# The last sections of a fused Fourier-mixing and attention kernel: output-projection chains issued two at a time on half the partitions each

## The chip, the cores and the metric

The kernel runs on one core of one Trainium2 chip. The metric is the device time of one launch in microseconds (us): the median of three runs is 1662.59, and they lie between 1661.75 and 1662.68. The core has five engines with an instruction queue each: TensorE (PE, matmuls, with weight loads shown apart as PEld), VectorE (DVE), ScalarE (ACT), GpSimd (POOL) and SyncE (SP, which here only issues transfers). Each queue runs in order.

## The reference

Two mixers work on the same 2048 x 512 input and are blended row by row with a gate.

```python
def _A_ref(x, dft_seq_re, dft_seq_im, dft_hid_re, dft_hid_im):
    a = jnp.einsum("bsd,ed->bse", x, dft_hid_re)
    b = jnp.einsum("bsd,ed->bse", x, dft_hid_im)
    return jnp.einsum("ts,bse->bte", dft_seq_re, a) - jnp.einsum("ts,bse->bte", dft_seq_im, b)

def _B_ref(x, wqkv, wo):
    B, S, D = x.shape
    H = 32; Dh = D // H
    ...                                  # q, k, v: [B, H, S, Dh]
    scores = jnp.einsum("bhqd,bhkd->bhqk", q, k) * Dh ** -0.5
    p = _softmax(scores, axis=-1)
    o = jnp.einsum("bhqk,bhkd->bhqd", p, v)
    return o.transpose(0, 2, 1, 3).reshape(B, S, D) @ wo

g = _sigmoid((x * gate_w).sum(-1, keepdims=True))
return g * _A_ref(...) + (1 - g) * _B_ref(...)
```

## The kernel before

Attention is done for 16 pairs of heads (p = 0 to 15). The queries are taken in two halves of 1024 (hf = 0, 1), the keys in 16 tiles of 128 (kt). One *unit* u is one (p, hf, kt); there are 512, numbered by 32 p + 16 hf + kt. A unit has four score matmuls (two blocks of 512 queries, two heads h), each on the 64 partitions that belong to its head (L798), four exponentials on ACT (L799) and one `values` call, four matmuls with 17 columns each that add into the PSUM bank `acc` (L844, and L806 for the last 16 units); the trace shows each of these as two. Two heads use different halves of the array, so their score matmuls run side by side. Everything else that PE has to do is put between the score matmuls: first maxima (L292) and the Fourier transform, and at the end the output projection.

The projection (`proj`) gives one chain of matmuls per block of 128 rows (a *qt*, eight per half hf) and group of weight rows `ct`: three matmuls for each ct, since operands are kept as a high and a low part. A chain adds up in one PSUM bank, and at its end `finish` (L668, on DVE) adds the scaled bank to the output row block `yp`; that reading frees the bank. `Chain.mm` (L469) issues one matmul on all 128 partitions, or with a `half` on 64 of them.

The order is written out by hand. Up to unit 491 it follows patterns in which each chain is cut in two halves of 64 partitions and mixed with score matmuls. From unit 492 on, which the diff touches, the loop at the end of the kernel takes two units at a time (called *iteration 492* and so on, up to 510): four score pairs, between the second and the third of them the chains that the table `whole` lists for that iteration, then two `values` calls, which belong to the two units before. The chains there are `first` (hf 0, ct 0 to 2, nine matmuls each), `third` (hf 1, ct 3), `early` and `last` (hf 0, ct 0 or 3; three matmuls each). They run on 128 partitions. PSUM has eight banks: seven in rings (`psS` banks 0 to 2, `psA` 3 to 5, `acc` 6) and `psD`. In the last iterations the score matmuls of head 0 use psS and those of head 1 psA, and the chains take psD, psS and psA in turn.

Beside this runs a *plan*: a table from units to steps (`at`), carried out at the start of an iteration. For the last group of heads (ct 3) of half hf 0 the steps are: `sums` (498) loads the softmax sums `rc` from the memory o_d; `last_block` step 0 (498) loads the raw outputs `o_raw`; `load_w15` (498) issues eight transfers `w`; `inverse` (500) takes the reciprocal of rc on DVE (L586) and stores it to r_d; step "sums" (500) loads it back, spread over partitions, as the second half of `o_raw`; step 1 (504) multiplies the two on POOL (L643); step 2 (506) splits the product in high and low parts on DVE (L629, L630), which the `last` chains use in iterations 508 and 510. What starts all this is the end of unit 495: `evacuate` copies acc on ACT (L825), adds it on POOL (L826) to `oe` and stores it to o_d (L829). `LastPair` treats the last pair of heads apart: `turn` (four small matmuls, L732, and DVE work L734 and L736) in iteration 506, `back` (a transposition, L742) in 508, `products` (L751) after the loop.

Of the kernel before, what the change touches and what calls it, by code (L numbers as in the profile page):

```python
# [9 lines left out]
F32 = mybir.dt.float32  # L10
# [5 lines left out]
P = 128  # L16
S = 2048
# [14 lines left out]
def mix_kernel(ctx: ExitStack, tc: tile.TileContext, xa_t, xa, wqkv, w_hid, w_seq, wo, gate_w, out):  # L32
# [5 lines left out]
    nc = tc.nc  # L38
# [26 lines left out]
                self.touch(self.of[id(t)][1])  # L65

    psS, psA = Ring(0, 1, 2), Ring(3, 4, 5)
    psO = Ring(6)
    psD = ctx.enter_context(tc.tile_pool(name="psD", bufs=1, space=PSUM))
    dram = ctx.enter_context(tc.tile_pool(name="dram", bufs=1, space=DRAM))  # L70
    const = ctx.enter_context(tc.tile_pool(name="const", bufs=1))
# [19 lines left out]
    g = const.tile([P, NT], F32, name="g")  # L91
    ng = const.tile([P, NT], F32, name="ng")
    omg = const.tile([P, NT], F32, name="omg")
    mx = [const.tile([P, 2, NT, 4], F32, name=f"mx{i}") for i in range(2)]
    nm = [const.tile([P, 16, 2], F32, name=f"nm{i}") for i in range(2)]
    nhl = [const.tile([P, 2, 16], F32R, name=f"nhl{i}") for i in range(2)]
# [23 lines left out]
    todo, loaded, behind = [], [], []  # L120
# [72 lines left out]
    with tc.tile_pool(name="qk", bufs=1, reuse_waits="tile") as pool:  # L193
# [38 lines left out]
        for tb in range(4):  # L232
# [141 lines left out]
    made, user = 0, None  # L374
# [383 lines left out]
    last_pairs = []  # L758
# [42 lines left out]
    def pv_last(u):  # L801
        blk, k2 = divmod(u - UNITS + 16, 8)
        pt = pts.pop(u)
        for j in range(4):
            x, h = divmod(j, 2)
            nc.tensor.matmul(acc[32 * j:32 * j + 17], vt[:, 2 * k2 + x, NP - 1, 16 * h:16 * h + 17], pt[:, j],  # L806
                             start=k2 == 0, stop=k2 == 7)
        if blk == 0 and k2 == 7:
            last_pairs.append(LastPair(0, [(psS, "s"), (psA, "a")]))
            last_pairs[0].copy(1)  # L810

    part, closed = [], False
# [69 lines left out]
    def at(u, f, *args):  # L882
        plan.setdefault(u, []).append(partial(f, *args))

    for hf in range(2):
        for ct in range(4):
            n = 3 if hf and ct == 3 else 4
            last = 32 * (4 * ct + n - 1) + 16 * (hf + 1)
            at(last + (4 if ct < 3 else 2), sums, hf, ct, n)
            at(last + (12 if ct < 3 else 4), inverse, hf, ct, n)  # L890
            if ct < 3:
                for half in range(2):
                    for step, du in enumerate((20, 24, 26)):
                        at(last + du + 8 * half, block, step, hf, ct, half)

    for p in range(1, NP):
        for h in range(2):
            at(32 * (p - 1) + 2 * h * (p > 1), load_stacks, p, [h])
    one, two, three = [(psD, "d")], [(psS, "s"), (psD, "d")], [(psS, "s"), (psA, "a"), (psD, "d")]
    at(456, load_yg, 0, range(3))  # L900
    at(481, load_yg, 0, range(3, 8))
    for step, u in enumerate((486, 490, 494)):
        at(u, last_block, step, 1, 3, nc.gpsimd)
    for step, u in ((0, 498), ("sums", 500), (1, 504), (2, 506)):
        at(u, last_block, step, 0, 4, nc.gpsimd)
    at(498, load_w15)
    lead = a_next

    def run_plan(u):
# [24 lines left out]
    streams = [stream(h) for h in range(2)]  # L934
# [74 lines left out]
            for i in range(n):  # L1009
                yield NINE, take(gen, 9)  # L1010

    first = proj(0, (0, 1, 2), one * 5 + two[:1] + one, range(7))
    run_plan(0)
    gate()
    hid, seq = real(), dft()
# [15 lines left out]
    maxima_left = False  # L1031

    run_plan(valued)
    for bank in (*three[:1], *three):
        scores(*next(streams[1][0]), bank)
    run_deferred()
    assert not any(a_left.values())
    third = proj(1, (3,), two)
    last = proj(0, (3,), three[1:] + three[:1], range(7))

    early, late = proj(0, (0,), one, (7,)), proj(0, (1, 2, 3), [(psS, "s")], (7,))
    whole = {492: ((first, 9),), 494: ((first, 6),), 496: ((first, 3), (third, 3)), 498: ((third, 6),), 500: ((third, 6),),
             502: ((third, 3),), 504: ((early, 3), (third, 3)), 506: ((third, 3),), 508: ((last, 9),), 510: ((last, 12),)}
    for u in range(valued + 2, UNITS, 2):
        run_plan(u)
        for i in range(4):
            if i == 2:
                for gen, n in whole[u]:
                    pump(gen, n)
                if u == 506:  # L1050
                    last_pairs[0].turn()
                elif u == 508:
                    last_pairs[0].back()
            for h in range(2):
                scores(u + i // 2, i % 2, h, three[h])
        values()
        values()
    last_pairs[0].products([(psS, "s"), (psA, "a"), (psA, "a"), (psD, "d")], range(4))
# [39 lines left out]
```

## Time and profile before

| | us |
|---|---|
| median of three runs | 1662.59 |
| the profiled execution, its own time | 1662.97 |
| its span, first to last instruction | 1661.1 |
| PE busy in the span | 1651.7 |
| first score matmul after the last pattern | 1595.96 |
| first score matmul of iteration 498 | 1612.13 |
| first matmul of `products`, after the loop | 1648.09 |
| last matmul starts | 1654.80 |

The page of the profile has the busy time of each engine, the span in slices, the chain of work that ended last, and the costliest groups of instructions. Its table of stretches gives the busy time of each engine between two times, and its timeline lists instructions in order of time: start, duration, engine, line, operation, output and inputs, count, and in brackets how long the engine had stood idle before and what ended that. Rows that begin with SPq are transfers being issued on SP. All times are counted from the start of the span. The loop that is changed takes the last 3.1% of it: from 1595.96 to 1648.09 is 52.1 us.

### The profile page before, as it was taken

To read this page: it belongs to the slowest core of one execution; us is meant where nothing else is said; L and a number is where in the kernel's file an instruction comes from. 1 tells how busy PE (TensorE), PEld (TensorE's weight loads), DVE (VectorE), ACT (ScalarE), POOL (GpSimd) and SP (SyncE) were. 2 spreads that over 40 slices of the span, in tenths; PEclk is the share of its full clock that TensorE was granted. 3 is DMA by queue.
4 is the path that set the end of the run, shared out by engine and by line. 5 is a ranking of instruction groups with operands and counts; after the bars stand their busy time and mean duration, and the time that the engine had idled before them with its cause. 6 is when DMAs were issued, how large, how long until landed. Compare 5 with 4: busy or idle time off the path is not lost.

```text
span 1661.1 us, 34392 instructions
## 1 busy us (share of the span) xinstructions
PE 1651.7 (99%) x13040; PEld 976.0 (59%) x13040; DVE 1383.3 (83%) x2361; ACT 1264.7 (76%) x2469; POOL 654.0 (39%) x615
## 2 busy tenths in 40 slices
PE   9999999999999999999999999999999999999998
PEld 7888755455555555555555555555555555544443
DVE  5439888888888888888888888888888888899954
ACT  5212388888888888888888887888788878889996
POOL 0202133344434355444343455544445456333330
PEclk9999999999999999999999999999999999999999
DMA  8973610514151342514147444315141535462114
GB/s 287 347 168 109 185 21 9 70 34 85 39 98 47 69 108 84 99 46 79 47 85 253 95 116 95 87 59 92 50 87 59 112 104 122 140 187 40 40 29 141
DMA packets 85245, 167.14 MB, mean 101 GB/s; under 512 B 22460, under 2 KB 22716, under 8 KB 81068
## 3 DMA queue, kind: packets, MB, share of 16 engines
q1 hardware_dynamic: 84648, 164.30, 39.2%
q8 instruction: 102, 1.67, 0.4%
q10 hardware_dynamic: 432, 0.66, 0.1%
q14 instruction: 63, 0.52, 0.1%
HBM read 109.67 MB, written 55.17 MB: 99 GB/s over the span
## 4 chain that ended last, share of the span: by engine, by line
PE 98%; DMA 1%; DVE 0%; POOL 0%; SPq 0%; ACT 0%; issue 0%; DVEq 0%; POOLq 0%; ACTq 0%
PE acc L844 28%; PE a L292 21%; PE s L798 19%; PE d L469 12%; PE s L383 3%; PE acc L798 3%; PE acc L292 2%; PE s L415 1%; PE d L383 1%; PE a L108 1%; PE a L107 1%; PE s L108 1%; PE s L107 1%; PE a L109 1%; PE s L109 1%; PE a L469 1%
## 5 line engine op out<-in xcount | busy, mean ns | idle before, releaser
L294 DVE TENSOR_REDUCE mx<-a 128x1 f32<-128x512 f32 x1834 | 1144.1, 683 | 158.3 <-PE a L292 115.0
L799 ACT ACTIVATE pt<-s 128x512 f32<-128x512 f32 x1762 | 933.2, 624 | 32.8 <-PE s L798 17.3
L292 PE MATMUL a<-ks,qs 64*128 64x512 f32 (+1 forms) x1834 | 679.3, 409 | 0.0
L469 PE MATMUL d<-xab,ch 64*128 64x512 f32 x2016 | 647.8, 396 | 0.0
L798 PE MATMUL s<-qs,ks 64*128 64x512 f32 (+1 forms) x1762 | 574.1, 395 | 0.9 <-DVE on L736 0.5
L826 POOL TENSOR_TENSOR oe<-oe,part 128x512 f32<-128x512 f32 x215 | 278.2, 1294 | 655.3 <-ACT part L825 650.3
L844 PE MATMUL acc<-pt,vt 128*17 128x512 f32 x3968 | 484.1, 596 | 0.0
L292 PEld LDWEIGHTS a<-ks,qs 64*128 64x128 f32 (+1 forms) x1834 | 325.6, 184 | 231.9 <-issue 122.5
L469 PE MATMUL d<-xab,cl 64*128 64x512 f32 x1008 | 399.3, 396 | 0.0
L469 PEld LDWEIGHTS d<-xab,ch 64*128 64x128 f32 x2016 | 366.5, 184 | 11.5
L798 PEld LDWEIGHTS s<-qs,ks 64*128 64x128 f32 (+1 forms) x1762 | 316.1, 184 | 80.5 <-ACT pt L799 28.2
L825 ACT COPY part<-acc 128x512 f32<-128x512 f32 x215 | 126.4, 588 | 185.7 <-issue 174.6
L844 PEld LDWEIGHTS acc<-pt,vt 128*17 128x17 f32 x3968 | 86.7, 96 | 224.2 <-issue 141.8
L469 PEld LDWEIGHTS d<-xab,cl 64*128 64x128 f32 x1008 | 185.6, 184 | 5.9
L454 POOL TENSOR_TENSOR cl<-craw,ch 128x512 fp32r<-128x512 f32 x126 | 162.2, 1287 | 10.1
L294 DVE TENSOR_REDUCE mx<-acc 128x1 f32<-128x512 f32 x214 | 147.8, 691 | 10.7
L799 ACT ACTIVATE pt<-acc 128x512 f32<-128x512 f32 x244 | 147.9, 606 | 0.0
L798 PE MATMUL acc<-qs,ks 64*128 64x512 f32 (+1 forms) x244 | 95.4, 391 | 0.0
L469 PE MATMUL d<-wre,xab 64*128 64x512 f32 x336 | 90.5, 402 | 0.0
L453 POOL CAST ch<-craw 128x512 fp32r<-128x512 f32 x126 | 77.3, 613 | 18.6 <-PE d L469 13.9
L469 PEld LDWEIGHTS d<-wre,xab 64*128 64x128 f32 x336 | 59.9, 184 | 40.7 <-issue 12.3
L292 PE MATMUL acc<-ks,qs 64*128 64x512 f32 (+1 forms) x214 | 83.1, 388 | 0.0
(174 smaller groups left out, 1212.7 us busy)
## 6 DMA issues: line engine op xcount, KB each, us to landing
craw<-w_seq SPq DMA_DIRECT2D x128, 256.0 KB
qk<-hl SPq DMA_DIRECT2D x32, 512.0 KB
qs<-qk SPq DMA_DIRECT2D x96, 128.0 KB
ks<-qk SPq DMA_DIRECT2D x96, 128.0 KB
b<-hl SPq DMA_DIRECT2D x16, 512.0 KB
xab<-b SPq DMA_DIRECT2D x16, 512.0 KB
o<-oe SPq DMA_DIRECT2D x62, 128.0 KB
oh<-nh SPq DMA_DIRECT2D x12, 512.0 KB
```

The costliest lines, as they stand in the source:

```text
L107: nc.tensor.matmul(ps, sh, mh, start=first, stop=False)
L292: nc.tensor.matmul(ps, qs[p % 2][r, qt * P:(qt + 1) * P], ks[p % 2][r, kb * 512:(kb + 1) * 512], start=True, stop=True)
L294: user = nc.vector.tensor_reduce(mx[p % 2][:, h, qt, kb:kb + 1], ps, AX.X, ALU.max)
L383: i = nc.tensor.matmul(ps, st[r], mv[r], start=not half and not j, stop=half == 1 and j == 11)
L453: nc.gpsimd.tensor_copy(h1, raw)
L454: nc.gpsimd.tensor_tensor(l1, raw, h1.bitcast(F32), ALU.subtract)
L469: i = nc.tensor.matmul(self.ps, st[r], mv[r], start=not self.begun, stop=stop)
L798: nc.tensor.matmul(ps, ks[p % 2][rr, kt * P:(kt + 1) * P], qs[p % 2][rr, q0:q0 + 512], start=True, stop=True)
L799: return nc.scalar.activation(pts[u][:, 2 * qb + h], ps, AF.Exp, bias=0.0, scale=DH ** -0.5)
L825: nc.scalar.copy(part[0], acc)
L826: nc.gpsimd.tensor_tensor(total, total, part[0], ALU.add)
L844: i = nc.tensor.matmul(acc[32 * j:32 * j + 17], v[:, 16 * h:16 * h + 17], pt[:, j], start=begin, stop=done or close)
```

## The change

Six things change, all after unit 491.

- Chains run in twos (`side_by_side`). Two chains x and y are taken together; in a first turn x runs on partitions 0 to 63 and y on 64 to 127, matmul by matmul in alternation, then the halves are swapped for a second turn. Each chain thus has twice as many matmuls on half the partitions.
- Between the turns stand score matmuls (the strings in `orders`: S is a pair of score matmuls, W three steps of a turn, w one), and the second turn waits for the first: a one-column memset `tick` on POOL waits for the last matmul of the first turn, and the first matmul of the second turn waits for that memset.
- The banks are dealt anew. Score matmuls take any of banks 0 to 4 (`psE`), chains alternate between psD and bank 5 (`psP`).
- The chains are spread anew over the iterations: 9, 5 and 4 slots of a pair for `first` in 492 to 496, six slots in each of 498 to 504, none in 506, twelve in 508 and in 510. In slots it was 9, 6, 6, 6, 6, 3, 6, 3, 9, 12; both sums are 66.
- In the plan `inverse` for hf 0 moves from 500 to 502, step "sums" of `last_block` from 500 to 502, `load_w15` from 498 to 504.
- `back` moves from iteration 508 to the start of 510.

```diff
     psS, psA = Ring(0, 1, 2), Ring(3, 4, 5)
+    psE, psP = Ring(0, 1, 2, 3, 4), Ring(5)
...
-            last_pairs.append(LastPair(0, [(psS, "s"), (psA, "a")]))
+            last_pairs.append(LastPair(0, [(psE, "s"), (psE, "a")]))
...
-            at(last + (12 if ct < 3 else 4), inverse, hf, ct, n)
+            at(last + (12 if ct < 3 else 4 + 2 * (hf == 0)), inverse, hf, ct, n)
...
+    side = [(psD, "d"), (psP, "a")]
...
-    for step, u in ((0, 498), ("sums", 500), (1, 504), (2, 506)):
+    for step, u in ((0, 498), ("sums", 502), (1, 504), (2, 506)):
         at(u, last_block, step, 0, 4, nc.gpsimd)
-    at(498, load_w15)
+    at(504, load_w15)
...
-    first = proj(0, (0, 1, 2), one * 5 + two[:1] + one, range(7))
+    first = proj(0, (0, 1, 2), one * 5 + side[::-1], range(7))
...
-    for bank in (*three[:1], *three):
-        scores(*next(streams[1][0]), bank)
+    for _ in range(4):
+        scores(*next(streams[1][0]), (psE, "s"))
...
-    third = proj(1, (3,), two)
-    last = proj(0, (3,), three[1:] + three[:1], range(7))
-    early, late = proj(0, (0,), one, (7,)), proj(0, (1, 2, 3), [(psS, "s")], (7,))
-    whole = {492: ((first, 9),), 494: ((first, 6),), 496: ((first, 3), (third, 3)), 498: ((third, 6),), 500: ((third, 6),),
-             502: ((third, 3),), 504: ((early, 3), (third, 3)), 506: ((third, 3),), 508: ((last, 9),), 510: ((last, 12),)}
+    third = proj(1, (3,), side)
+    last = proj(0, (3,), side, range(7))
+    early, late = proj(0, (0,), side[1:], (7,)), proj(0, (1, 2, 3), [(psS, "s")], (7,))
+
+    def behind(i, other):
+        tc.add_manual_dep(i.ins, other.ins.name,
+                          mybir.DependencyInfo(mybir.DependencyClass.Sync, mybir.DependencyReason.DATA))
+
+    def side_by_side(x, y):
+        both = x(), y()
+        for turn in range(2):
+            for n, pair in enumerate(zip(*both)):
+                for k, (chain, st, mv, after) in enumerate(pair):
+                    end = turn == 1 and n == len(both[0]) - 1
+                    i = chain.mm(st, mv, turn ^ k, end)
+                    if turn and not n and not k:
+                        behind(i, user)
+                    if end and after:
+                        after()
+                if not turn and n == len(both[0]) - 1:
+                    user = nc.gpsimd.memset(tick, 0.0)
+                    behind(user, i)
+                yield
...
+    begun = beside((of(first, 9), of(first, 9)))
+    whole = {492: begun, 494: begun, 496: begun}
+    for u in range(498, 504, 2):
+        whole[u] = beside((of(third, 3), of(third, 3)))
+    whole[504] = beside((of(third, 3), of(early, 3)))
+    whole[508] = beside((of(third, 3), of(last, 3)), (of(last, 3), of(last, 3)))
+    whole[510] = beside((of(last, 3), of(last, 3)), (of(last, 3), of(last, 3)))
+    orders = {492: "W S W S W S S", 494: "S W S S w w S", 496: "S w w S S w w S", 506: "S S turn S S", 508: "W S S W W S S W", 510: "W S S W W S S W"}
     for u in range(valued + 2, UNITS, 2):
         run_plan(u)
-        for i in range(4):
-            if i == 2:
-                for gen, n in whole[u]:
-                    pump(gen, n)
-                if u == 506:
-                    last_pairs[0].turn()
-                elif u == 508:
-                    last_pairs[0].back()
+        if u == 510:
+            last_pairs[0].back()
+        i = 0
+        for slot in orders.get(u, "S W S S W S").split():
+            if slot == "turn":
+                last_pairs[0].turn()
+                continue
+            if slot != "S":
+                for _ in range(3 if slot == "W" else 1):
+                    next(whole[u])
+                continue
             for h in range(2):
-                scores(u + i // 2, i % 2, h, three[h])
+                scores(u + i // 2, i % 2, h, (psE, "s"))
+            i += 1
         values()
         values()
```

How the instructions stand is shown at three places. Line numbers of the changed kernel are two higher than those of the profile (L469 is L471, L643 is L645, L798 is L800, L826 is L828). The first place is PE in iteration 498, from the fourth score matmul to the `values` calls; `s` and `a` are PSUM banks of the rings, `d` is psD. Before:

```order
L798 MATMUL a<-qs_973,ks_975 128x512
L469 MATMUL d<-wo_hl,o_lno 128x512 x3
L469 MATMUL s<-wo_hl,o_lno 128x512 x3
L798 MATMUL s<-qs_973,ks_975 128x512
L798 MATMUL a<-qs_973,ks_975 128x512
L798 MATMUL s<-qs_973,ks_975 128x512
L798 MATMUL a<-qs_973,ks_975 128x512
L806 MATMUL acc<-pt,vt 17x512 x8
```

Now, from the end of the first turn into the second; there are six chain matmuls in each turn:

```order
L471 MATMUL a<-wo_hl,o_lno 128x512
L471 MATMUL d<-wo_hl,o_lno 128x512
L471 MATMUL a<-wo_hl,o_lno 128x512
L800 MATMUL s<-qs_974,ks_976 128x512 x4
L471 MATMUL d<-wo_hl,o_lno 128x512
L471 MATMUL a<-wo_hl,o_lno 128x512
L471 MATMUL d<-wo_hl,o_lno 128x512
```

Two chains of three matmuls each stood in one block on 128 partitions; now they alternate on halves, with two score pairs between the turns.

The second place is the end of POOL's queue: `oe` is the sum of unit 495's `evacuate` (the last L826), `o_raw` the products of hf 1 and then hf 0. Before:

```order
L314 TENSOR_TENSOR nhl_200<-nm_198,nhl_200 128x16
L643 TENSOR_TENSOR o_raw<-o_raw 128x1024
L826 TENSOR_TENSOR oe<-oe,part 128x512
L643 TENSOR_TENSOR o_raw<-o_raw 128x1024
L666 TENSOR_TENSOR yp_19914<-yp_19914,few 128x512
```

Now:

```order
L645 TENSOR_TENSOR o_raw<-o_raw 128x1024
L1062 MEMSET tick 128x1
L828 TENSOR_TENSOR oe<-oe,part 128x512
L1062 MEMSET tick 128x1 x3
L645 TENSOR_TENSOR o_raw<-o_raw 128x1024
L1062 MEMSET tick 128x1 x5
L668 TENSOR_TENSOR yp_19915<-yp_19915,few 128x512
```

Nine memsets came in: one for the pair of `first` chains, three for iterations 498 to 502, and behind the product of hf 0 those of 504, 508 (two) and 510 (two).

The third place is PE in iteration 508. Before, its chains and what follows:

```order
L469 MATMUL a<-wo_hl,o_l 128x512 x3
L469 MATMUL d<-wo_hl,o_l 128x512 x3
L469 MATMUL s<-wo_hl,o_l 128x512 x3
L742 MATMUL a<-ident,on_22213 128x128
L798 MATMUL s<-qs_973,ks_975 128x512
```

Now, the last step of the first pair's second turn, the first turn of the second pair, and the score matmuls behind it:

```order
L471 MATMUL a<-wo_hl,o_lnh 128x512
L471 MATMUL d<-wo_hl,o_l 128x512
L471 MATMUL a<-wo_hl,o_l 128x512
L471 MATMUL d<-wo_hl,o_l 128x512
L471 MATMUL a<-wo_hl,o_l 128x512
L471 MATMUL d<-wo_hl,o_l 128x512
L471 MATMUL a<-wo_hl,o_l 128x512
L471 MATMUL d<-wo_hl,o_l 128x512
L800 MATMUL s<-qs_974,ks_976 128x512 x4
```

Three chains had three banks; now the second pair follows the first directly, in the same two banks.

More of the change, by code (lines that the diff above doesn't have):

```diff
@@ L93, in mix_kernel @@
     omg = const.tile([P, NT], F32, name="omg")
+    tick = const.tile([P, 1], F32, name="tick")
     mx = [const.tile([P, 2, NT, 4], F32, name=f"mx{i}") for i in range(2)]
@@ new lines, in of, with beside @@
+    def of(gen, n):
+        return lambda: [next(gen) for _ in range(n)]
+    def beside(*pairs):
+        for x, y in pairs:
+            yield from side_by_side(x, y)
+    begun = beside((of(first, 9), of(first, 9)))
[5 more added lines that the diff above has]
+    whole[510] = beside((of(last, 3), of(last, 3)), (of(last, 3), of(last, 3)))
```

## The prediction

> **What bounds the kernel now.** I read the page first, then the table of stretches over the last 110 us, then the timeline of PE from 1595 on, and last those of POOL, SP, DVE and ACT in the same stretch.
>
> ```profile
> span 1661.1 us, 34392 instructions
> PE 1651.7 (99%) x13040; PEld 976.0 (59%) x13040; DVE 1383.3 (83%) x2361; ACT 1264.7 (76%) x2469; POOL 654.0 (39%) x615
> 1610.00:1620.00 10.00, 10.00 (x68) 4.16 (x68) 1.93 (x3) 9.08 (x18) 1.29 (x1) 1.00 0.14 31
> ```
>
> The stretch (PE, PEld, DVE, ACT, POOL, granted clock, DMA share, GB/s) lies in the changed loop: PE is full, ACT next at 91%, DVE and POOL nearly free, the clock at 1.00. So a slot saved on PE is worth its length until ACT or a wait takes over. Next, one iteration of the loop on PE:
>
> ```profile
> 1602.60 0.49 PE L798 MATMUL s<-qs,ks 64*128 64x512 f32 x1
> ...
> 1603.26 1.67 PE L469 MATMUL d<-wo_hl,o_hl 128*128 128x512 f32 x6
> 1604.86 0.50 PE L798 MATMUL s<-qs,ks 64*128 64x512 f32 x1
> ...
> 1605.53 1.91 PE L844 MATMUL acc<-pt,vt 128*17 128x512 f32 x16
> 1607.37 0.50 PE L798 MATMUL s<-qs,ks 64*128 64x512 f32 x1
> ```
>
> From start to start: two score pairs 0.66, six chain matmuls on 128 partitions 1.60, two pairs 0.67, the values 1.84; 4.77 in all. Against it a block of the last patterns, where halves of chains and scores are mixed on 64 partitions:
>
> ```profile
> 1585.38 0.50 PE L469 MATMUL d<-wo_hl,o_hl 64*128 64x512 f32 x1
> 1585.38 0.50 PE L292 MATMUL a<-ks,qs 64*128 64x512 f32 x1
> 1585.72 0.39 PE L469 MATMUL d<-wo_hl,o_hl 64*128 64x512 f32 x1
> 1585.95 0.39 PE L469 MATMUL d<-wo_hl,o_hl 64*128 64x512 f32 x1
> ...
> 1587.90 1.05 PE L844 MATMUL acc<-pt,vt 128*17 128x512 f32 x8
> ```
>
> The block holds 20 matmuls (9 L469, 11 others), two at a time: ten slots, 0.23 apart (1585.72 to 1585.95). It takes 2.52, so entering and leaving it costs 2.52 - 2.31 = 0.21. The old iteration has ten slots too: 4.77 - 2.31 - 1.84 = 0.62 of overhead, for three blocks (64, 128, 64 partitions). Two waits of PE and the first exponential complete the picture:
>
> ```profile
> 1622.06 0.50 PE L798 MATMUL s<-qs,ks 64*128 64x512 f32 x1 [0.34 <-DVE yp L668]
> 1636.39 0.46 PE L798 MATMUL s<-qs,ks 64*128 64x512 f32 x1 [0.54 <-DVE on L736]
> 1596.63 1.14 ACT L799 ACTIVATE pt<-s 128x512 f32<-128x512 f32 x2
> 1604.16 0.60 ACT L799 ACTIVATE pt<-s 128x512 f32<-128x512 f32 x1
> 1604.64 0.62 ACT L799 ACTIVATE pt<-a 128x512 f32<-128x512 f32 x1
> ```
>
> Both waits are for a bank that DVE frees late. ACT starts an exponential every 0.48, so eight of an iteration need 3.84.
>
> **What the change removes.** An iteration with six chain slots becomes one block: 2.52 + 1.84 = 4.36, or 0.41 less. That holds for nine of the ten iterations (492 to 504, 508, 510): 3.7. In 506 the small matmuls of `turn` keep the three blocks. The number of slots is unchanged (66). The two waits fall away too, 0.88: the 0.34 arose because a score matmul had to reuse the bank of a chain, which now has banks of its own, and the 0.54 because `turn` stood on DVE behind the split of a late product, which now lies under the stall worked out below. Gain 3.7 + 0.9 = 4.6.
>
> **The stall in 504.** The second turn of a pair waits for a memset on POOL, and POOL's queue is in order. Ahead of the memset of 504 stands the product of hf 0, which waits for a chain of transfers. What waits behind it on PE is a score pair and the values; behind these, ACT. The chain, across the queues:
>
> ```profile
> 1612.13 0.49 PE L798 MATMUL s<-qs,ks 64*128 64x512 f32 x1
> 1612.98 1.29 POOL L826 TENSOR_TENSOR oe<-oe,part 128x512 f32<-128x512 f32 x1 [11.82 <-ACT part L825]
> 1614.30 1.16 SPq L829 DMA_DIRECT2D o<-oe  x2
> 1617.27 1.52 SPq L572 DMA_DIRECT2D rc<-o  x2
> 1620.16 3.80 SPq L706 DMA_DIRECT2D w<-wo  x8
> 1620.23 0.55 DVE L586 RECIPROCAL rc<-rc 128x64 f32<-128x64 f32 x1 [4.99 <-DMA rc<-o]
> 1624.09 1.19 SPq L589 DMA_DIRECT2D r<-rc  x2
> 1626.10 1.19 SPq L606 DMA_DIRECT2D o_raw<-r  x2
> 1630.71 2.38 POOL L643 TENSOR_TENSOR o_raw<-o_raw 128x1024 f32<-128x1024 f32 x1 [16.44 <-DMA o_raw<-r]
> ```
>
> Iteration 498 began at 1612.13; the reciprocals' input was there 8.10 later; the reciprocal ended at 1620.78, but SP was busy with eight `w` transfers until 1623.96; from the issue of r to the product 6.62, and the product 2.38.
>
> After the change 498 begins earlier by 3 x 0.41 for three iterations and 3 x 0.23 for three slots fewer before it (18, not 21): at 1610.2. Scores have five banks where scores and chains shared seven, and the 28 exponentials from 1596.63 on need 13.4, up to 1610.1; with PE never far ahead of ACT I take 0.9 of waiting for banks (bounds 0 and 1.4, the latter if each iteration to 496 loses a whole exponential's 0.48). So 498 begins at 1611.1, and every step follows:
>
> - rc is there at 1611.1 + 8.1 = 1619.2. In front of the reciprocal DVE now has the two finishes of 500. Iteration 498 itself stalls: its memset stands behind the sum L826, which ends at 1611.1 + 2.14, or 1613.3 with the memset; PE comes after six slots and half the entry, at 1612.6: 0.8 lost. So 500 begins at 1616.3, its chains end nine slots later, at 1618.5, and two finishes (0.2 after PE, 0.69 apart, rows below) hold DVE until 1620.1.
> - The reciprocal ends at 1620.65; SP is free, since the w transfers are queued later; r and o_raw take 6.62, to 1627.3; the product ends at 1629.7, the memset at 1629.85.
> - PE reaches the second turn of 504 after two iterations of 4.36 and 1.5: at 1626.5.
>
> The stall is 1629.85 - 1626.5 = 3.3. Bounds: 2.4 if the reciprocal does not stand behind the finishes; 5.7 if moving w saves nothing and the product ends 20.96 after the start of 498, as now.
>
> A page of the Trainium skill, "DMA: Bandwidth & Descriptors", section "Anatomy of one DMA", gives a transfer about 2.0 us plus its bytes at 436 GB/s. By it the four hops would be some 9.6 us where the rows have 12.55 (2.97, 2.96, 2.01, 4.61), and the stall an estimated 0.4. The trace does not agree: only the third hop comes near 2.0.
>
> **Second pairs in 508 and 510.** The second pair starts in the banks of the first, right behind it, and must wait for DVE to finish them.
>
> ```profile
> 1626.79 0.96 PE L469 MATMUL d<-wo_hl,o_hl 128*128 128x512 f32 x3
> 1627.59 0.85 PE L469 MATMUL s<-wo_hl,o_lnh 128*128 128x512 f32 x3
> 1627.79 0.75 DVE L668 SCALAR_TENSOR_TENSOR yp_ks<-d,omg,yp_ks 128x512 f32<-128x512 f32 x1 [3.31 <-PE d L469]
> 1628.48 0.75 DVE L668 SCALAR_TENSOR_TENSOR yp<-s,omg,yp 128x512 f32<-128x512 f32 x1
> 1621.27 0.74 DVE L668 SCALAR_TENSOR_TENSOR yp<-s,omg,yp 128x512 f32<-128x512 f32 x1
> ```
>
> DVE starts 0.20 after the chain's last slot (1627.59 to 1627.79), the second finish follows 0.69 later and takes 0.75, and PE goes on 0.05 after a finish (1622.01 to 1622.06). Both chains now end together, so the second bank is free 0.20 + 0.69 + 0.75 + 0.05 = 1.7 later, and PE has nothing else to issue. Twice 1.7 is 3.4; at least twice 1.0, if only the first bank counted. Before, the fourth chain of 510 found a third bank and DVE kept pace.
>
> **The other memsets and small things.**
>
> ```profile
> L1091 POOL MEMSET const-float32-0.0<- 128x1 f32 x1 | 0.1, 99 | 0.2 <-issue 0.2
> 1622.06 0.18 PEld L798 LDWEIGHTS s<-qs,ks 64*128 64x128 f32 x1 [1.26 <-DVE yp L668]
> ```
>
> A one-column memset takes 0.10. With 0.20 from PE to a consumer and 0.05 back a turn is answered in 0.35, and two score slots give 0.46. The weight load of 0.18 may have to follow the answer: between 0 and 0.1 at seven places, I take 0.3 in all. The other moved steps cost nothing on the path: the eight `w` transfers (3.80 on SP) go out behind o_raw at about 1624, under the stall, and are wanted by `products` some 25 us later; the two o_raw transfers only change places with them; the transposition is one matmul as before.
>
> **The sum.** Gain 4.6; loss 3.3 (504) + 0.8 (498) + 3.4 (508, 510) + 0.9 (banks) + 0.3 (memsets) = 8.7. Net +4.1 on the profiled execution's 1662.97, or 1667.1; that execution is 0.38 above the median of the runs, so the median comes to 1666.7. What lies behind the loop is not touched. This case's own range takes the lower bounds together (504 -0.9, banks -0.9, pairs -1.4, memsets -0.3) and the upper ones (+2.4, +0.5, +0.4): 1663.2 to 1670.0.
>
> **The rivals.** A measurement of this kernel tells about 0.2% from no change, which is 3.3: below 1659.3 is faster, above 1665.9 slower.
>
> *The product is in time* (no stall in 504): 1666.7 - 3.3 = 1663.4, the same. It needs o_raw 3.3 sooner. For it: the DMAs were loaded with w while r was written, and no longer are. Against it: the o_raw hop alone has 4.61 with w already done.
>
> *Both kinds of wait fail* (product in time and the second pairs covered): 1663.4 - 3.4 = 1660.0, and with the bank waits gone 1659.1, faster. It needs DVE to free two banks in no time; only the switches saved speak for it.
>
> *The answer is slower than two score slots*: if POOL and the weight load need 0.70 in place of 0.35, seven turns lose 0.24 each, 1.7 in place of 0.3: 1668.1. Against it is the 0.10 of the memset.
>
> *The clock falls in the stall.* PE's last row and the end of the table of stretches:
>
> ```profile
> 1654.80 0.39 PE L751 MATMUL d<-w,o 32*128 32x512 f32 x1
> 1659.00:1660.00 1.00, 0.00 (x0) 0.00 (x0) 0.00 (x0) 0.00 (x0) 0.00 (x0) 0.81 0.64 240
> 1660.00:1661.10 1.10, 0.00 (x0) 0.00 (x0) 0.00 (x0) 0.00 (x0) 0.00 (x0) 0.50 0.00 0
> ```
>
> PE ends at 1655.2 and the clock is halved at about 1659.6, 4.4 later. A stall of that length, 1.1 more than mine, and the 2.8 of PE work behind it at half the rate give 1666.7 + 1.1 + 2.8 = 1670.6. A page of the Trainium skill, "TensorE: Matmul & The Clock Gate", Part 1, has the gate close after one idle window of about 3.4 us, which runs free; by it a stall of 3.3 is just too short, and one that fills a window would cost an estimated half of 3.4, or 1668.4. No wait of that length inside this trace tells.
>
> *The halves don't run side by side*: then 66 slots become 132, 15 more: 1682. The two rows at 1585.38 speak against it.
>
> **Chances.** My case 0.52 (0.42 of it above 1665.9), product in time 0.22, faster 0.08, slow answer 0.10, clock 0.06, not side by side 0.02. Slower is 0.42 + 0.10 + 0.06 + 0.02 = 0.60, same 0.10 + 0.22 = 0.32, faster 0.08. The range from 1661.0 to 1670.0 takes in the product in time with 2 to spare, and leaves out most of the faster case and the clock.
>
> **What would show it.** In the timeline of the changed kernel PE should wait some 3 us in 504 with POOL's memset named, 0.8 in 498 with the same, and twice 1.7 for L670 (L668 now) in 508 and 510; blocks of ten slots should take 2.5. SP should issue r within 0.1 of the reciprocal's end. I am wrong if POOL's product begins before 1624, if PE never stands for a finish, or if a ten-slot block takes more than 3.

## The result and the profile after

The changed kernel takes 1670.84 us (median of six runs, 1669.31 to 1671.6) against 1662.55 for the kernel before in the same session (six runs, 1661.75 to 1663.6): a ratio of 1.005, 95% interval 1.0039 to 1.0061. It is slower by 8.3, twice the forecast 4.1, and above the range, which ended at 1670.0. Its profiled execution took 1671.6, 8.63 more than that of before; the forecast of 4.1 was made between the two profiled executions, and that is how they are compared here.

All of it lies in the loop: from the first score behind the last pattern to the first matmul of `products` it is 60.96 (1595.53 to 1656.49) where it was 52.13. First the page of the changed kernel and its table of stretches (PE, PEld, DVE, ACT, POOL, granted clock, DMA share, GB/s):

```profile
span 1669.8 us, 34532 instructions
PE 1654.9 (99%) x13106; PEld 982.6 (59%) x13106; DVE 1383.0 (83%) x2361; ACT 1264.0 (76%) x2469; POOL 655.3 (39%) x624
1600.00:1610.00 10.00, 10.00 (x77) 4.55 (x81) 3.43 (x6) 9.20 (x20) 0.76 (x2) 1.00 0.01 2
1620.00:1630.00 10.00, 6.74 (x56) 3.53 (x48) 2.02 (x4) 7.79 (x16) 2.19 (x2) 0.95 0.68 158
1630.00:1640.00 10.00, 9.60 (x52) 3.83 (x56) 3.79 (x7) 5.09 (x11) 0.29 (x2) 0.71 0.01 2
```

PE is still "99%", and the page alone shows nothing. The stretches do: from 1620 on PE stands, and from 1630 on it is busy, but at a granted clock of 0.71 with fewer matmuls (52 where the first stretch has 77). Next the timeline of PE: every matmul with a wait ahead of it, the `values` blocks that close the iterations 496 to 506, and two sets of four scores.

```profile
1609.12 1.91 PE L846 MATMUL acc<-pt,vt 128*17 128x512 f32 x16
1613.19 0.50 PE L471 MATMUL d<-wo_hl,o_lno 64*128 64x512 f32 x1 [0.40 <-POOL tick L1062]
1614.32 1.91 PE L808 MATMUL acc<-pt,vt 128*17 128x512 f32 x16
1618.78 1.91 PE L808 MATMUL acc<-pt,vt 128*17 128x512 f32 x16
1623.21 1.91 PE L808 MATMUL acc<-pt,vt 128*17 128x512 f32 x16
1626.08 0.66 PE L800 MATMUL s<-qs,ks 64*128 64x512 f32 x4
1630.35 0.79 PE L471 MATMUL d<-wo_hl,o_lnh 64*128 64x512 f32 x1 [3.61 <-POOL tick L1062]
1632.35 3.56 PE L808 MATMUL acc<-pt,vt 128*17 128x512 f32 x16
1637.67 1.43 PE L800 MATMUL s<-qs,ks 64*128 64x512 f32 x4
1639.03 1.91 PE L808 MATMUL acc<-pt,vt 128*17 128x512 f32 x16
1643.93 0.50 PE L471 MATMUL a<-wo_hl,o_l 64*128 64x512 f32 x1 [0.82 <-DVE yp L670]
1644.59 0.50 PE L471 MATMUL d<-wo_hl,o_l 64*128 64x512 f32 x1 [0.16 <-DVE yp L670]
1651.87 0.50 PE L471 MATMUL a<-wo_hl,o_l 64*128 64x512 f32 x1 [0.84 <-DVE yp_qs L670]
1652.53 0.50 PE L471 MATMUL d<-wo_hl,o_l 64*128 64x512 f32 x1 [0.16 <-DVE yp_qs L670]
```

From one `values` block to the next an iteration takes 5.20 in 498, 4.46 and 4.43 in 500 and 502, then 9.14 and 6.68 in 504 and 506. Every wait that was forecast is there, by its releaser: the memset in 498 and in 504, and the finishes in 508 and 510. Two things were not forecast. The `values` block of 504 lasts 3.56, not 1.91, and four scores in 506 last 1.43 where those at 1626.08 last 0.66. The chain in front of the memset, on POOL, SP and DVE:

```profile
1611.82 1.28 POOL L828 TENSOR_TENSOR oe<-oe,part 128x512 f32<-128x512 f32 x1 [11.06 <-ACT part L827]
1613.12 1.15 SPq L831 DMA_DIRECT2D o<-oe  x2
1617.30 1.21 SPq L574 DMA_DIRECT2D rc<-o  x2
1619.32 0.74 DVE L670 SCALAR_TENSOR_TENSOR yp<-a,omg,yp 128x512 f32<-128x512 f32 x1
1620.07 0.55 DVE L588 RECIPROCAL rc<-rc 128x64 f32<-128x64 f32 x1
1620.65 1.19 SPq L591 DMA_DIRECT2D r<-rc  x2
1627.91 2.34 POOL L645 TENSOR_TENSOR o_raw<-o_raw 128x1024 f32<-128x1024 f32 x1 [5.87 <-DMA o_raw<-r]
1630.19 0.10 POOL L1062 MEMSET tick<- 128x1 f32 x1
```

The reciprocal stands right behind the two finishes (the second is shown), r is issued 0.03 after its end, at the forecast 1620.65, and PE goes on 0.06 after the memset. Last, the stretch of the stall cut where the clock changes, in steps of 3.41:

```profile
1625.49:1628.90 3.41, 1.25 (x12) 0.79 (x8) 0.00 (x0) 3.04 (x6) 0.99 (x1) 1.00 0.97 220
1628.90:1632.31 3.41, 1.96 (x8) 1.17 (x8) 0.28 (x1) 0.00 (x0) 1.39 (x2) 0.50 0.16 25
1632.31:1635.72 3.41, 3.41 (x18) 0.49 (x16) 2.95 (x4) 1.09 (x2) 0.00 (x0) 0.50 0.00 0
1635.72:1639.13 3.41, 3.36 (x24) 1.92 (x24) 0.56 (x3) 3.14 (x7) 0.00 (x0) 1.00 0.02 5
```

The clock falls at 1628.90, only 2.2 after PE's last matmul ended (1626.08 + 0.66 = 1626.74), and is back at 1635.72. PE works from 1630.35 to 1635.72, 5.37, at half the rate: 2.7 lost.

### The profile page after: what moved, and what is told of

The parts are those of the page before. It is cut to its first block, busy times and chain, and to the rows that moved or that the text cites. A ratio compares the mean times of both kernels' runs of the same rounds, so it can differ in the third digit from the quotient of the medians.

```text
span 1669.8 us, 34532 instructions
## 1 busy us (share of the span) xinstructions
PE 1654.9 (99%) x13106; PEld 982.6 (59%) x13106; DVE 1383.0 (83%) x2361; ACT 1264.0 (76%) x2469; POOL 655.3 (39%) x624
## 4 chain that ended last, share of the span: by engine, by line
PE 98%; DMA 1%; DVE 0%; ACT 0%; POOL 0%; issue 0%; SPq 0%; DVEq 0%; POOLq 0%; ACTq 0%
PE acc L846 28%; PE a L294 21%; PE s L800 19%; PE d L471 13%; PE s L385 3%; PE acc L800 3%; PE acc L294 2%; PE s L417 1%; PE d L385 1%; PE acc L808 1%; PE a L110 1%; PE a L109 1%; PE s L110 1%; PE s L109 1%; PE a L111 1%; PE s L111 1%
## 5 line engine op out<-in xcount | busy, mean ns | idle before, releaser
L801 ACT ACTIVATE pt<-s 128x512 f32<-128x512 f32 x1804 | 950.2, 624 | 38.1 <-PE s L800 28.7
L471 PE MATMUL d<-xab,ch 64*128 64x512 f32 x2016 | 647.9, 396 | 0.0
L800 PE MATMUL s<-qs,ks 64*128 64x512 f32 (+1 forms) x1804 | 578.9, 395 | 0.0
L828 POOL TENSOR_TENSOR oe<-oe,part 128x512 f32<-128x512 f32 x215 | 278.4, 1295 | 654.0 <-ACT part L827 640.8
L471 PE MATMUL d<-xab,cl 64*128 64x512 f32 x1008 | 399.4, 396 | 0.0
L471 PEld LDWEIGHTS d<-xab,ch 64*128 64x128 f32 x2016 | 366.5, 184 | 11.9
L800 PEld LDWEIGHTS s<-qs,ks 64*128 64x128 f32 (+1 forms) x1804 | 321.0, 185 | 78.4 <-ACT pt L801 29.7
L471 PEld LDWEIGHTS d<-xab,cl 64*128 64x128 f32 x1008 | 185.6, 184 | 6.0
L800 PE MATMUL acc<-qs,ks 64*128 64x512 f32 (+1 forms) x244 | 95.4, 391 | 0.0
L471 PE MATMUL d<-wre,xab 64*128 64x512 f32 x336 | 90.5, 402 | 0.0
L471 PEld LDWEIGHTS d<-wre,xab 64*128 64x128 f32 x336 | 59.9, 184 | 40.7 <-issue 12.3
```

Of the source, the lines that this page charges most:

```text
L471: i = nc.tensor.matmul(self.ps, st[r], mv[r], start=not self.begun, stop=stop)
L800: nc.tensor.matmul(ps, ks[p % 2][rr, kt * P:(kt + 1) * P], qs[p % 2][rr, q0:q0 + 512], start=True, stop=True)
L801: return nc.scalar.activation(pts[u][:, 2 * qb + h], ps, AF.Exp, bias=0.0, scale=DH ** -0.5)
L828: nc.gpsimd.tensor_tensor(total, total, part[0], ALU.add)
```

## The experiments

The diffs are against the changed kernel unless another is named. Where a ratio is given, it is to the kernel before, timed in the same session.

**The stall.** First the product of hf 0 is put one iteration later, so that it is issued on POOL behind the memset of 504.

```diff
-    for step, u in ((0, 498), ("sums", 502), (1, 504), (2, 506)):
+    for step, u in ((0, 498), ("sums", 502), (1, 506), (2, 506)):
```

> The changed kernel with one plan entry moved: the product of hf 0 on POOL is issued at unit 506 instead of 504, so it stands behind the memset of iteration 504 and not ahead of it. Queue theory: PE's wait of 3.6 us in 504 goes, PE stays at full clock, and the rest of 504 takes 2.8 us in place of 5.5; the product then ends near 1630, before 508 needs it. Time 1670.8 - 3.6 - 2.7 = 1664.5. Lateness theory (the transfers are what is late, and the wait only moves): the chains of 508 wait instead, and the time stays above 1668. Mix theory (the half clock comes from running halves side by side, not from the wait): the wait goes but the clock still falls, about 1667.

Measured: 1665.1 (ten runs), ratio 1.0013 (1.0004 to 1.0022). PE no longer stands in 504, the clock stays at 1.00, and 504 and 506 together take 9.48 where the changed kernel has 15.82. The 6.3 between them is the wait of 3.6 and the clock's 2.7. So one memset behind one product carries the larger part of the loss.

Next all the memsets are put on DVE; POOL then has nothing that PE waits for.

```diff
-                    user = nc.gpsimd.memset(tick, 0.0)
+                    user = nc.vector.memset(tick, 0.0)
```

> The changed kernel with all nine memsets on DVE instead of POOL. Queue theory: the wait of 504 goes (3.6 and 2.7 for the clock), and the 0.8 of 498 too, since the sum of the unit before holds POOL and not DVE: 1670.8 - 7.1 = 1663.7. If a turn on DVE is answered later than on POOL because finishes stand ahead of it, 498 and 500 to 502 lose up to 0.7 each and the time is about 1665.5.

Measured: 1663.63 (ten runs), ratio 1.0005 (0.9995 to 1.0014). What its timeline of PE has of waits in 510 (508 has the same two; there are no others):

```profile
1643.89 0.50 PE L471 MATMUL a<-wo_hl,o_l 64*128 64x512 f32 x1 [0.84 <-DVE yp_qs L670]
1644.55 0.50 PE L471 MATMUL d<-wo_hl,o_l 64*128 64x512 f32 x1 [0.15 <-DVE yp_qs L670]
```

The waits in 498 and in 504 are both gone, and the second pairs' waits are untouched, as they should be: those are for banks. It is 1.5 below the kernel with the product moved: in the profiles 0.6 lies in 498 (4.58 in place of 5.19) and 0.3 in 508 and 510 together (7.54 and 7.76 in place of 7.69 and 7.95). Where the rest lies was not traced.

**The clock.** Does the fall cost something of its own, or is it only how the stall looks? Fourteen more score matmuls into a bank that nobody reads are put into 504's wait, so that PE stands less while the wait itself is not shortened.

```diff
-    orders = {492: "W S W S W S S", ...}
+    orders = {492: "W S W S W S S", 504: "S W S S busy W S", ...}
...
+            if slot == "busy":
+                t = psE.tile([P, 512], F32, "s")
+                for _ in range(14):
+                    nc.tensor.matmul(t, ks[1][:64, :P], qs[1][:64, :512], start=True, stop=True)
```

> The changed kernel with 14 more matmuls of 64 partitions in iteration 504, ahead of the second turn, into a free score bank that nobody reads: PE works where it had waited (14 x 0.23 = 3.2 us of 3.6), all else as it was. Idle theory: PE still starts the second turn when the memset comes, near 1630.3, but the granted clock stays at 1.00, and what follows in 504 takes 2.8 us in place of 5.5: 1670.8 - 2.7 = 1668.1. Mix theory: the clock falls all the same, 1670.8.

Measured: 1670.08 (four runs), ratio 1.0043 (1.0028 to 1.0057), which by time alone can't be told from the changed kernel. The profile can tell:

```profile
1629.07 2.37 POOL L645 TENSOR_TENSOR o_raw<-o_raw 128x1024 f32<-128x1024 f32 x1 [6.51 <-DMA o_raw<-r]
1631.53 0.49 PE L471 MATMUL d<-wo_hl,o_lnh 64*128 64x512 f32 x1 [0.79 <-POOL tick L1062]
1632.66 1.91 PE L808 MATMUL acc<-pt,vt 128*17 128x512 f32 x16
```

The clock stays at 1.00, and from the second turn to the end of the `values` block 504 takes 2.97 (1631.53 to 1632.66 + 1.84) where the changed kernel takes 5.50: 2.5 for the clock. But in this execution the product came 0.64 later after the sum, and the loop began 0.53 later; that gave 1.2 back. So the expected time was missed by 2.0, and the cost of the clock is shown by the rows, not by the times. The same with seven matmuls (`range(7)`):

> The changed kernel with 7 in place of 14 extra matmuls ahead of the second turn of 504: PE works 1.6 us of the wait and stands about 2.3. In the changed kernel the clock fell 2.2 us after the last matmul. If 2.2 us of standing always does it, the clock falls just before the second turn and the rest of 504 takes 5.5 us; if it depends on where the standing lies in a longer stretch, the clock may stay at 1.00 and the rest takes 2.9.

Measured: 1670.14 (one run). PE stands only 1.56 here, and the clock falls all the same, 1.04 after PE has gone on:

```profile
1629.75 0.49 PE L471 MATMUL d<-wo_hl,o_lnh 64*128 64x512 f32 x1 [1.56 <-POOL tick L1062]
```

Its table of stretches, cut where the clock changes:

```profile
1627.38:1630.79 3.41, 1.85 (x12) 1.02 (x10) 0.04 (x1) 0.83 (x2) 2.32 (x2) 1.00 0.41 63
1630.79:1634.20 3.41, 3.41 (x18) 0.49 (x16) 3.19 (x4) 1.08 (x2) 0.00 (x0) 0.50 0.02 5
1634.20:1637.61 3.41, 3.35 (x24) 1.88 (x24) 0.56 (x3) 3.10 (x7) 0.00 (x0) 1.00 0.00 0
```

A clock that falls while PE works is hardly a delay counted from the last matmul (2.6 here, 2.2 in the changed kernel). It looks like a look back over 3.41: in the stretch ahead of the fall PE was busy for 1.85 of it, 54%. Half speed then lasts one stretch of 3.41, not two. To test this, the changed kernel was profiled once more, as it is.

> The changed kernel itself, profiled a second time, to see what decides when the clock falls in 504. Theory: the clock is set anew every 3.41 us on a grid that runs free of the program, and falls where TensorE was busy for less than about 0.6 of the stretch before; in this profile the times at which it falls and rises in 504, and the time at which it falls behind the last matmul of the kernel, then differ by whole multiples of 3.41 us, and the fall comes at another distance behind the last matmul than the 2.2 us of the first profile, wherever the grid lies. Rival: the clock falls a fixed time, 2.2 us, after TensorE went idle, and comes back 6.8 us later, as in the first profile. The time by both is about 1670.8 us, by the theory up to 1.7 lower where TensorE's wait falls into two stretches that are both mostly busy.

Measured: 1672.31 (one run). The stretches around its stall, and the stretch behind the kernel's last matmul in which the clock falls again:

```profile
1625.78:1629.20 3.42, 1.08 (x10) 0.67 (x6) 0.00 (x0) 2.98 (x6) 0.23 (x1) 1.00 1.03 249
1629.20:1632.61 3.41, 1.21 (x6) 1.03 (x8) 0.00 (x0) 0.00 (x0) 2.14 (x2) 0.50 0.26 47
1632.61:1636.02 3.41, 3.41 (x22) 0.63 (x18) 2.90 (x4) 1.08 (x2) 0.00 (x0) 0.50 0.00 0
...
1666.50:1667.00 0.50, 0.00 (x0) 0.00 (x0) 0.00 (x0) 0.00 (x0) 0.00 (x0) 0.74 1.02 381
```

A mean clock of 0.74 in a stretch of 0.50 puts the last fall at 1666.74. From 1629.20 that is 37.54, eleven times 3.413. The first profile of the changed kernel gives 1666.45 - 1628.90 = 37.55, eleven times again; the kernel with seven matmuls 1664.93 - 1630.79 = 34.14, ten times. So the clock is set on a grid of 3.413. The distance from the last matmul, which the theory wanted different, is 2.35 against 2.2: too near to tell anything alone. What the run adds is a second surprise: the stall is 4.54 here, since the product began 17.03 after the sum's start, not 16.09.

**The plan.** Its moves alone, in the kernel before:

```diff
-            at(last + (12 if ct < 3 else 4), inverse, hf, ct, n)
+            at(last + (12 if ct < 3 else 4 + 2 * (hf == 0)), inverse, hf, ct, n)
...
-    for step, u in ((0, 498), ("sums", 500), (1, 504), (2, 506)):
+    for step, u in ((0, 498), ("sums", 502), (1, 504), (2, 506)):
...
-    at(498, load_w15)
+    at(504, load_w15)
```

> The kernel before with the three moved plan steps alone (reciprocal and reload at 502, the eight w transfers at 504); chains, banks and order as before. My account: SP issues r right behind the reciprocal, the product ends about 3 us earlier (1630 instead of 1633.1), and the waits of 0.34 and 0.54 of PE go: 1662.55 - 0.9 = 1661.7. Rival: the reciprocal only changes places with the finishes and the waits come back elsewhere: 1662.5. Were the moved steps a loss by themselves, it would be above 1664.

Measured: 1661.72 (ten runs), ratio 0.9993 (0.9983 to 1.0002). By the times alone that can't be told from the kernel before. In the profile the product begins at 1627.75, 3.0 earlier than in the kernel before (0.5 of it because the loop began earlier), and both of PE's old waits are gone. And the reverse, the same three lines taken back in the changed kernel:

> The changed kernel with the plan's moves alone taken back: the inverse sums and the reciprocal stand at iteration 500 again and the last weights at 498. Theory (the sums then end later, and the product of hf 0, which POOL's memset of 504 stands behind, ends later too): the product ends about 21 us after the start of 498 or later, TensorE stands about 5 us in 504 in place of 3.6, the clock falls there and stays at half for one or two stretches of some 3.4 us: 1673 to 1674.5 us against 1670.8 of the changed kernel. Rival: the plan's moves do nothing for the product and the time stays at 1670.8.

Measured: 1673.94 (four runs), ratio 1.0078 (1.0062 to 1.0093). The product and the wait behind it, in its timeline:

```profile
1630.42 2.34 POOL L645 TENSOR_TENSOR o_raw<-o_raw 128x1024 f32<-128x1024 f32 x1 [7.26 <-DMA o_raw<-r]
1632.85 0.79 PE L471 MATMUL d<-wo_hl,o_lnh 64*128 64x512 f32 x1 [4.99 <-POOL tick L1062]
```

The stretches around it:

```profile
1625.65:1629.07 3.42, 2.21 (x20) 1.18 (x12) 0.00 (x0) 2.76 (x6) 0.00 (x0) 1.00 0.63 149
1629.07:1632.48 3.41, 0.00 (x0) 0.00 (x0) 0.00 (x0) 0.69 (x2) 2.06 (x1) 1.00 0.05 10
1632.48:1635.90 3.42, 3.05 (x16) 1.49 (x20) 1.37 (x3) 0.94 (x2) 0.32 (x2) 0.50 0.00 0
```

The moves of the plan are the good part of the change: without them the product begins 18.1 after the start of the sum (16.1 and 17.0 in the two executions with them), and the stall is 4.99. The clock tells more. This time it falls 4.6 after the last matmul (1632.48 against 1627.23 + 0.64): the stretch in which PE's wait began still had 65% of work and did not count, and the empty one behind it did. With 2.2, 2.6 and 4.6 a fixed delay is excluded. The longer stall lost one stretch of half speed instead of two.

**The banks.** With the memsets on DVE, the chains of 508 and 510 get four banks (psD, 3, 4, 5), and the scores of these two iterations keep banks 0 to 2.

```diff
-                    user = nc.gpsimd.memset(tick, 0.0)
+                    user = nc.vector.memset(tick, 0.0)
...
+    psQ, psR = Ring(3), Ring(4)
+    four = [(psD, "d"), (psQ, "a"), (psR, "a"), (psP, "a")]
...
-    last = proj(0, (3,), side, range(7))
+    last = proj(0, (3,), four, range(7))
...
-                scores(u + i // 2, i % 2, h, (psE, "s"))
+                scores(u + i // 2, i % 2, h, (psS if u > 506 else psE, "s"))
```

> The kernel with memsets on DVE and four banks for chains in 508 and 510, the order of matmuls as in the changed kernel. Bank theory: the second pair starts at once (3.4 us less), but four score matmuls in a row on three banks wait for the first exponential, about 0.6 us four times: 1663.6 - 3.4 + 2.4 = 1662.6. Rival (DVE's finishes are the limit, not the banks): the wait stays, 1663.6.

Measured: 1663.55 (ten runs), ratio 1.0006 (0.9997 to 1.0015), 1 above the expectation. The waits for DVE are gone, and four others have come:

```profile
1635.40 0.49 PE L800 MATMUL s<-qs,ks 64*128 64x512 f32 x1 [0.51 <-ACT pt L801]
...
1643.10 0.49 PE L800 MATMUL s<-qs,ks 64*128 64x512 f32 x1 [0.45 <-ACT pt L801]
```

Four scores one after the other find only three banks, and the last waits until ACT has emptied one. The brackets count only the time in which PE stands. The fourth score starts 1.08 to 1.14 after the first of the three where one slot of 0.23 would do; these four delays of 0.85 to 0.91 make 3.5, not the 2.4 expected, and take back what the banks gain. So the two pairs are woven in addition, with one score pair behind every three steps.

```diff
+    def woven(*pairs):
+        both = [side_by_side(x, y) for x, y in pairs]
+        for turn in range(2):
+            for pair in both:
+                for _ in range(3):
+                    next(pair)
+                    yield
...
-    whole[508] = beside((of(third, 3), of(last, 3)), (of(last, 3), of(last, 3)))
+    whole[508] = woven((of(third, 3), of(last, 3)), (of(last, 3), of(last, 3)))
...
-    orders = {..., 508: "W S S W W S S W", ...}
+    orders = {..., 508: "W S W S W S W S", ...}
```

(510 likewise.)

> The kernel with memsets on DVE, and in 508 and 510 four banks for chains (psD and banks 3, 4 and 5; scores keep 0 to 2), the two pairs woven: first turn of one, first turn of the other, second turns, a score pair after each. Bank theory: the two waits of 1.7 us for L670 go, 1663.6 - 3.4 = 1660.2. Rival: with three banks for scores PE waits for exponentials instead (a pair of scores needs 0.96 us of ACT and comes every 0.92), 0.5 us for each of eight pairs: 1664. If the waits were only work that PE must do anyway, 1663.6.

Measured: 1660.98 (11 runs), ratio 0.999 (0.9981 to 0.9999). No wait of PE is left in 508 and 510. Last, in this kernel, `turn` of 506 gets bank 5 in place of a turn in the scores' ring.

```diff
-            last_pairs.append(LastPair(0, [(psE, "s"), (psE, "a")]))
+            last_pairs.append(LastPair(0, [(psP, "a"), (psE, "a")]))
```

> The woven kernel with the four chain banks, in which the pattern and the clears of 504's third chains now lie in their own bank 5 (shared with chains that are long done by then) and no more in the ring of the score banks. Theory: what made the scores of 506 wait was that the clears of the third chains took a place in that ring and ScalarE had to empty it first; with a bank of its own that wait is gone and 506 shrinks from 5.0 us to about 4.4: about 1660.4 us against 1661.0 of the woven kernel. Rival: the scores of 506 wait for ScalarE's exponentials anyway, with the ring or without: 1661.0.

Measured: 1660.19 (11 runs), ratio 0.9991 (0.9982 to 1.0): the times can't tell it from the woven kernel. In the profiles the scores behind `turn` shrink from 1.43 to 0.94, the woven kernel's row first:

```profile
1630.08 1.43 PE L800 MATMUL s<-qs,ks 64*128 64x512 f32 x4
```

```profile
1630.02 0.94 PE L800 MATMUL s<-qs,ks 64*128 64x512 f32 x4
```

506 takes 4.52 in place of 5.01. So the ring carries 0.5 of what these scores lose over 0.66, and the last 0.3 was not the ring's; its cause was not tried.

## Why the prediction was half right

The direction held, and so did the waits that make up most of the sum, but the sum was 4.5 short between the profiled executions. The step that failed is the rival "the clock falls in the stall". It got a chance of 0.06 because I read the one fall that the trace of before has, 4.4 after the last matmul, as the length that a stall must have, found mine 1.1 shorter, and priced the fall at 2.8 with a longer stall added. The price was right (2.7, or 2.5 by the run with fourteen matmuls), the condition was not. What decides is how much PE worked in the stretch of the grid that is just over: the clock fell behind stretches with 1.25, 1.08 and 1.85 of 3.41. The 4.4 that I had read were the end of a stretch with 70% of work (1652.80 to 1656.22) and the empty one behind it. Beside my own forecast of a 3.3 us stall it should have been likelier than not.

The same rival drew on the Trainium skill, "TensorE: Matmul & The Clock Gate", Part 1: one idle window of about 3.4 us, free running. The runs agree with the window's length and with its running free (ten and eleven whole multiples). They do not agree that it must be idle: 54% of work in it was not enough. The advice of the Trainium skill on the same page, "Why this matters for your kernels", no gap over about 3 us, would have let the 1.56 pass. The measurement decides.

Point by point; the forecasts for 506, 508 and 510 are worked out from the prediction's slots:

| step | forecast | measured in the profile | off by |
|---|---|---|---|
| start of 498 | 1611.1 | 1610.96 | -0.1 |
| 498, with a loss of 0.8 | 5.16 | 5.20 | |
| 500 and 502 | 2 x 4.36 | 4.46 + 4.43 | 0.2 |
| issue of r | 1620.65 | 1620.65 | |
| PE stands in 504 | 3.3 | 3.61 | 0.3 |
| clock in 504 | 0 | 2.7 | 2.7 |
| 506 | 4.2 | 5.02 | 0.8 |
| 508 and 510, with the second pairs | 15.0 | 7.69 + 7.93 | 0.6 |
| all memsets | 0.3 | in the rows above | -0.3 |

The last column adds up to 4.2. `products` began 4.3 later than forecast (1656.49 against 1648.09 + 4.1), and the other 0.2 of the 4.5 lie behind the loop.

**The stall.** Its mechanism, POOL's queue in order with the product ahead of the memset, is shown by the two runs that take one or the other away. The start of the product was forecast at 1627.3 and is 1627.91. That 0.6 is in the hop from r to o_raw (2.66 where the kernel before has 2.01); but a second execution of the same kernel had a stall of 4.54, so the 0.3 says little, and that it is so small is in part luck. The stall of 0.4 that I worked out from the Trainium skill, "DMA: Bandwidth & Descriptors", section "Anatomy of one DMA", does not count: that section gives its 2.0 us for transfers issued on GpSimd, and the four hops are issued on SP. With all the bytes that the hops move (256, 32, 32 and 512 KB) the sum by those figures would also be an estimated 10 us, not 9.6.

**The hop that moved and did not matter.** From the issue of o to that of rc I had taken over 2.97 from before; it is 4.18 (1613.12 to 1617.30). The two finishes in front of the reciprocal hid it. In the second execution it was 4.54, and there the reciprocal waited 0.44 for rc. Why the transfer lands later was not tried.

**The second pairs.** In the profile the first matmul into the second bank comes at 1644.59 where the slots alone would give 1642.94: 1.65. In the woven kernel the two iterations are 1.36 and 1.40 shorter than in the kernel with the memsets on DVE, so two waits of 1.65 are worth 2.8 when they are woven away, not 3.4.

**The saving.** I took PE as the bound of an iteration and worked out 4.36 from its ten slots. Iterations 494 and 496 have nine and eight, which would make 4.13 and 3.90; they take 4.42 and 4.43. Rows of ACT, and one of PE from 496, show another bound:

```profile
1602.64 4.03 ACT L801 ACTIVATE pt<-s 128x512 f32<-128x512 f32 x8 [0.40 <-PE s L800]
1607.06 4.03 ACT L801 ACTIVATE pt<-s 128x512 f32<-128x512 f32 x8 [0.39 <-PE s L800]
1608.69 0.50 PE L800 MATMUL s<-qs,ks 64*128 64x512 f32 x1
1621.15 4.03 ACT L801 ACTIVATE pt<-s 128x512 f32<-128x512 f32 x8 [0.43 <-PE s L800]
```

It is not ACT's work alone, since ACT stands 0.4 in every iteration until the first scores behind the `values` block come. It is a loop through both engines. Five banks hold five scores, so the eighth score of an iteration needs the bank that the third exponential empties. In 496 the first exponential starts at 1607.06, the first three take 1.58, and the eighth score starts at 1608.69. The `values` follow at 1609.12 and take 1.84, and then come the next first scores. With ten slots PE's own work is about as long (4.46 and 4.43), and its rows in 500 and 502 show no wait. There about 0.09 of what is above 4.36 lies in the first step of the second turn, which takes 0.32 where a slot takes 0.23; in 508 and 510 it takes 0.31 to 0.34 in each of the four second turns. Why was not tried.

The losses ahead of 498 are larger than the 0.9 that I put down: 0.3 and 0.5 in 494 and 496, and 0.35 in 492 (6.58 where 6.64 less 0.41 was forecast), 1.2 in all. That 498 began on time is luck: in this execution the loop began 0.43 earlier than in that of before.

**506.** I had seen that scores lose two banks, and priced it ahead of 498 alone. I overlooked that `turn` takes its bank from the same ring, so that four scores behind it wait for ACT, which first has to copy. Giving it a bank of its own won 0.5 back.

**The rivals.** "The product is in time" fell with the stall; moved on purpose it gave 1665.1 where I had worked out 1663.4, since the losses of 506 and of the other iterations are left. "The answer is slower" would have cost 0.24 in each turn, and "not side by side" some 1.4 in each iteration of six slots; 500 and 502 are 0.10 and 0.07 over the forecast, and PE goes on 0.06 after the memset.

## What to carry to other kernels

Price a forecast stall of TensorE twice: its own length, and the half clock behind it. Here 1.56 us of standing was enough for a fall, since a stretch of 3.41 us with 54% of work was followed by one, and each stretch at half speed costs up to 1.7. A wait that one engine answers for another should not be put into the in-order queue of an engine that waits for a transfer; one line that moved the memsets to DVE won some 7 of the 8.3 back. When PE's slots are thinned out, look for a loop through the next engine: here nine and eight slots took as long as ten, since five banks made the last scores wait for the third exponential. And when banks are dealt anew, every user of the ring counts, the small ones too.

## What the runs showed that was not expected

The clock is set on a grid of 3.413 us that lies elsewhere in each execution, and the stretch just over decides, as far as the twelve profiles of this case show. Stretches in which PE was busy for 32%, 37% and 54% were followed by a fall, those at half speed with 35% and 57% by more of it, and one with 65% by none. The share of busy time is not quite the measure: one stretch with 1.75 of 3.41 (51%), at the end of the run with the plan undone, was followed by none; its row:

```profile
1663.20:1666.61 3.41, 1.75 (x17) 0.86 (x15) 2.65 (x5) 0.95 (x2) 0.88 (x1) 1.00 0.21 79
```

The twelve profiles together bear this out. Cut on the grid from the last fall of each backwards, they have 15 stretches at full clock with no more than 37% of work, most of them at the end of the kernel, and a fall stands behind every one; none stands behind a stretch with 61% or more. Between lie three: the 51% above and 52% near the start of the run with fourteen matmuls (7.72 to 11.13) without a fall, the 54% with one. What is counted beside the busy time was not tried.

Because of the grid a longer stall can cost less clock than a shorter one: 4.99 lost one stretch at half speed, 3.61 two.

The path of transfers from the sum to the product is uncertain by about 1 us: from the start of the one to that of the other 16.09 and 17.03 in two executions of the same kernel, and 15.93 to 17.05 in seven others that leave these steps as they are. A stall at the end of such a path can't be forecast any closer.
